# Decode attention and FFN on one core: weight loads with other layouts, a fourth buffer for K and for its transposes, and one score bank

## The chip, the cores and the metric

The kernel runs on one core of a Trainium2 chip. The metric is the device time of one execution in microseconds (us); six runs gave a median of 737.5 us, from 734.01 to 742.04. The core has a matrix engine (TensorE, PE in the profile; its weight loads are PEld), a vector engine (VectorE, DVE), a scalar engine (ScalarE, ACT), a general engine (GpSimd, POOL) and a sync engine (SP) that here issues every DMA. Each works through its own instructions in order and waits for others on semaphores. The data in HBM is moved by 16 DMA engines into the on-chip memory SBUF; TensorE writes its results into PSUM, which has 8 banks of 512 fp32 columns on 128 partitions.

## The reference

One decode step for 8 sequences. Layer norm, attention of one query token over a cache of 4096 keys, output projection, residual; then layer norm, an FFN with the mish activation, residual. All inputs are bfloat16.

```python
# x: (8, 1, 448)   k_cache, v_cache: (8, 8, 4096, 256)   wq: (448, 4096)   wo: (4096, 448)
# w1: (448, 1792)  b1: (1792,)  w2: (1792, 448)
q = (layernorm(x) @ wq)                  # 16 query heads of 256, two for each of 8 KV heads
scores = einsum("bhqd,bhkd->bhqk", q, k) * 256 ** -0.5
o = einsum("bhqk,bhkd->bhqd", softmax(scores), v)
h = x + o @ wo
hh = layernorm(h) @ w1 + b1
out = h + (hh * tanh(softplus(hh))) @ w2
```

K and V together are 268 MB; everything else is about 11 MB.

## The kernel before

**Pairs and groups.** The work is cut into 64 pairs (sequence b, KV head g), pair i having b = i % 8 and g = i // 8. Eight pairs with the same g form group j. Every pair needs 2.097 MB of K and 2.097 MB of V.

**One pair.** `kndma` loads K into one of three buffers `K_nat`, with the keys spread over the partitions (each partition takes 32 consecutive keys, 16 KB). `pe_T(i)`, called T(i) in the text, transposes it on TensorE in 64 matmuls against an identity (L609): 8 tiles of 1024 columns, each into one of three PSUM banks `kTp_ps`. `evac_task` copies each tile into one of three buffers `kT`, on ScalarE (L431) for every third tile and on VectorE (L436) for the other two. Tile t waits until tile t - 3 has been copied. `pe_qk(i)` then multiplies the transposed K with the two queries of the pair, 64 matmuls (L628) into the group's score bank. There are two score banks, `S_flat`, used by the groups in turn. `pe_pv(i)` multiplies V, in one of four buffers `vS`, with the weights of the softmax, 64 matmuls (L672), and ScalarE copies the output (L417).

**One group.** When the eight pairs of a group have their scores, a softmax chain goes back and forth between the engines. First half: VectorE takes the maxima (L480), TensorE transposes them (L643), VectorE reduces them (L486, L488), TensorE spreads them over the partitions (L646), VectorE copies (L491) and subtracts them from the scores (L493, which reads the score bank and signals `S_SCONS`). Then ScalarE takes the exponential (L403). Second half: VectorE sums (L501), TensorE sums over partitions (L652), VectorE takes the reciprocal (L504, L506), TensorE spreads it (L654) and VectorE scales (L511, L513, which signals `S_ET`). `pe_qtmm(g)` computes the queries of a KV head from wq (L586), `pe_attn(g)` multiplies the group's output with its part of wo (L688) and VectorE adds it (L527).

**The order.** Every task has a key, and each engine runs its tasks in the order of the keys: T(i) at i - 1.95, qk(i) at i, pv(i) at i + 11.5, the queries of KV head g at 8g - 0.7, the first half of the chain of group j at 8(j+1) - 0.42 on TensorE, its second half at 8(j+1) + 0.15. So T runs two pairs ahead of qk, and pv eleven pairs behind it. TensorE's order is, again and again: T(k), pv(k-13), qk(k-1), T(k+1) and so on.

**The loads.** All are issued by SP, in the order of keys of their own: K(i) at i - 2.55, V(i) at i + 10.5, wq of KV head g at 8g - 2.2 (two buffers), wo, then b1 at 58.8 and w1 and w2 at 62.05. Before each of them SP waits for its buffer: K(i) until the tiles of T(i-3) have been copied (`wait_evacs_before`, L250), V(i) until pv(i-4) is done (`S_PVDONE`), w1 and w2 until every tile of every T has been copied, since they go into the buffers of K. A load at the head of this order that must wait holds back all loads behind it. Between K(63) and the twelve last V loads, V(52) to V(63), stand w1 and w2.

**The weights' layouts.** wq comes in eight slices of 512 columns with row c x 112 + p on partition p, so 448 rows of 1 KB each. w1 is laid out the same way (448 rows of 3584 B), w2 with row c x 128 + p on partition p (1792 rows of 896 B), b1 as single elements of 2 B. The matmuls of the FFN's first layer are at L713, of its second at L721, and L718 is 36 matmuls without use between them.

Of the kernel before, what the change touches and what calls it, by code (L numbers as in the profile page):

```python
# [7 lines left out]
AF = mybir.ActivationFunctionType  # L8
AX = mybir.AxisListType

NKTP = 3
KN_ENGINES = ("sp", "sp", "sp")
V_ENGINE = "sp"
W_ENGINE = "sp"
N_WARM = 36
DSPLIT = False
EVAC_ENG = ("act", "dve", "dve")


def bass_sequential_preLN__gqa_block_cached__dense_activation_mish__decode_kernel(  # L20
# [43 lines left out]
    scale = float(Dh) ** -0.5  # L64
    EPS = 1e-5
    NKB = 3
    NVB = 4
    LAG = GP + 3

    def pair_bg(i):  # L70
# [3 lines left out]
    with ctx:  # L74
# [9 lines left out]

        kT = [sb([P, 2, Sk], dt.bfloat16) for _ in range(NKB)]
        vS = [sb([P, KH, KL * Dh], dt.bfloat16) for _ in range(NVB)]
        NKN = 3
        K_nat = [sb([P, KH, KL * Dh], dt.bfloat16) for _ in range(NKN)]
        wqbuf = [sb([DC, NDC, GW], dt.bfloat16) for _ in range(2)]
        KNSZ = KH * KL * Dh  # L90
        if NDC * F <= KNSZ and NFC * D <= KNSZ:
            w1_v = K_nat[0][0:DC, :, :].rearrange("p kh x -> p (kh x)")[:, 0:NDC * F].rearrange("p (c n) -> p c n", c=NDC)
# [32 lines left out]
        rstd = sb([B, 1], dt.float32)  # L125
        xnT_sb = sb([DC, NDC, B], dt.bfloat16)
        hnT_sb = sb([DC, NDC, B], dt.bfloat16)
        hb = sb([P, NFC, B], dt.float32)
        hmin = sb([P, NFC, B], dt.float32)
        hmax = sb([P, NFC, B], dt.float32)  # L130
        ea = sb([P, NFC, B], dt.float32)
        eb = sb([P, NFC, B], dt.float32)
        m_s1 = sb([P, NFC, B], dt.float32)
        m_num = sb([P, NFC, B], dt.float32)
        m_b2 = sb([P, NFC, B], dt.float32)
        m_den = sb([P, NFC, B], dt.float32)
        m_rden = sb([P, NFC, B], dt.float32)
        m_t = sb([P, NFC, B], dt.float32)
        actT = sb([P, NFC, B], dt.bfloat16)
        eps_t = sb([P, 1], dt.float32)  # L140
        lnv = sb([B, 1], dt.float32)

        S_flat = [ps([P, 512], dt.float32) for _ in range(2)]
        o_ps = ps([P, 512], dt.float32)
        misc_ps = ps([P, 512], dt.float32)
        p0_ps = ps([P, 512], dt.float32)
# [12 lines left out]
        qT_ps = misc_ps[:, 256:256 + NHC * B].rearrange("p (c b) -> p c b", c=NHC)  # L159
        xnT_ps = p0_ps[0:DC, 0:NDC * B // 2].bitcast(dt.bfloat16).rearrange("p (c b) -> p c b", c=NDC)  # L160
        attn_ps = p0_ps[0:B, 64:64 + D]
        h1T_ps = S_flat[1][:, 0:NFC * B].rearrange("p (c b) -> p c b", c=NFC)

        S_X = sem("s_x")
        S_WQ = [sem(f"s_wq{n}") for n in range(2)]
        S_V = [sem(f"s_v{n}") for n in range(NVB)]
        S_KN = [sem(f"s_kn{n}") for n in range(NKN)]
        S_WOB = [sem(f"s_wob{n}") for n in range(2)]
# [53 lines left out]
        def key_qtmm(g):  # L222
            return B * g - 0.7
# [45 lines left out]
        def w_events(eng):  # L269
            def wodma(g):  # L270
                if g >= 2:
                    eng.wait_ge(S_ATT, g - 1)
                eng.dma_start(
                    out=wobuf[g % 2][:, :, :],
                    in_=A_wo[g * GW:(g + 1) * GW, :].rearrange("(c p) n -> p c n", p=P),
                ).then_inc(S_WOB[g % 2], 16)

            def w12(_):
                wait_evacs_before(eng, NTBP * NP)
                eng.dma_start(out=w1_v, in_=B_w1.rearrange("(c p) f -> p c f", p=DC)).then_inc(S_W2, 16)  # L280
                eng.dma_start(out=w2_v, in_=B_w2.rearrange("(c p) n -> p c n", p=P)).then_inc(S_W2, 16)

            def b1load(_):
                with nc.allow_non_contiguous_dma(reason="tiny b1 transposed load"):
                    eng.dma_start(out=b1_sb[:, :], in_=B_b1.rearrange("(c p) -> p c", p=P)).then_inc(S_W2, 16)

            ev = []
            for g in range(Hkv):
                ev.append((min(key_attn(g), NP + LAG) - 4.0, 2, g, wodma))
            ev.append((key_T(NP - 1) + 1.0, 3, 0, w12))  # L290
            ev.append((key_qtmm(Hkv - 1) + 3.5, 4, 0, b1load))
            return ev
# [21 lines left out]
        def sp_prog(sp):  # L314
            def xload(_):
                sp.dma_start(out=x_bf[:, :], in_=A_x.rearrange("b o d -> (b o) d")).then_inc(S_X, 16)

            def wqload(g):
                if g >= 2:
                    sp.wait_ge(S_QTMM, g - 1)  # L320
                sp.dma_start(
                    out=wqbuf[g % 2][:, :, :],
                    in_=A_wq[:, g * GW:(g + 1) * GW].rearrange("(c p) n -> p c n", p=DC),
                ).then_inc(S_WQ[g % 2], 16)

            events = [(-10, 0, 0, xload)]
            for g in range(Hkv):
                events.append((key_qtmm(g) - 1.5, 5, g, wqload))
            for i in range(NP):
                if KN_ENG(i) == "sp":  # L330
                    events.append((key_T(i) - 0.6, 0, i, lambda i_: kndma(sp, i_)))
                if V_ENGINE == "sp":
                    events.append((key_pv(i) - 1.0, 1, i, lambda i_: vdma(sp, i_)))
            if W_ENGINE == "sp":
                events += w_events(sp)
            events.sort(key=lambda e: (e[0], e[1], e[2]))
            for key, kind, a, fn in events:
                fn(a)
            sp.wait_ge(S_H2, 1)
            sp.dma_start(out=out.rearrange("b o d -> (b o) d"), in_=h2_bf[:, :]).then_inc(S_OUT, 16)  # L340
            sp.wait_ge(S_OUT, 16)
# [223 lines left out]
        def pe_phase0a(pe):  # L565
            pe.wait_ge(S_XN, 1)
            pe.wait_ge(S_CONST, 1)
            for kc in range(NDC):
                ins = pe.matmul(xnT_ps[:, kc, :], lhsT=xn_bf[:, kc * DC:(kc + 1) * DC], rhs=ident_bf[0:B, 0:B],
                                is_transpose=True, start=True, stop=True)  # L570
            ins.then_inc(S_P0A, 1)

# [2 lines left out]
        def pe_qtmm(g):  # L575
            def f(pe):
                if g == 0:
                    pe.wait_ge(S_XNT, 1)
                pe.wait_ge(S_WQ[g % 2], 16 * (g // 2 + 1))
                ncb = n_chainB_before(key_qtmm(g))  # L580
                if ncb > 0:
                    pe.wait_ge(S_ET, ncb)
                for cc in range(4):
                    c = 4 * g + cc
                    for kc in range(NDC):
                        ins = pe.matmul(qT_ps[:, c, :], lhsT=wqbuf[g % 2][:, kc, cc * P:(cc + 1) * P],  # L586
                                        rhs=xnT_sb[:, kc, :], start=(kc == 0), stop=(kc == NDC - 1))
                ins.then_inc(S_QTMM, 1)
            return f
# [1 line left out]
        for g in range(Hkv):  # L591
            at("pe", key_qtmm(g), pe_qtmm(g))

        def pe_T(i):
            def f(pe):
                if i == 0:
                    pe.wait_ge(S_CONST, 1)
                pe.wait_ge(S_KN[i % NKN], 16 * NDMA * (i // NKN + 1))
                kn = K_nat[i % NKN]
                for tl in range(NTBP):  # L600
                    t = i * NTBP + tl
                    half, nb = divmod(tl, NTB)
                    if t >= NKTP:
                        wait_evac_of(pe, t - NKTP)
                    for jj in range(8):
                        blk = nb * 8 + jj
                        kh, kl = divmod(blk, KL)
                        c0 = kl * Dh + half * P
                        ins = pe.matmul(kTp_v[t % NKTP][:, jj * P:(jj + 1) * P], lhsT=kn[:, kh, c0:c0 + P],  # L609
                                        rhs=ident_bf[:, :], is_transpose=True, start=True, stop=True)  # L610
                    ins.then_inc(S_TB, 1)
            return f

        def pe_qk(i):
            b, g = pair_bg(i)
            j = i // GP
            c0 = (i % GP) * REP

            def f(pe):
                if i % GP == 0 and j >= 2:  # L620
                    pe.wait_ge(S_SCONS, j - 1)
                if i % B == 0:
                    pe.wait_ge(S_QT, g + 1)
                wait_evacs_before(pe, NTBP * (i + 1))
                kbuf = kT[i % NKB]
                for blk in range(NBLK):
                    for half in range(2):
                        ins = pe.matmul(  # L628
                            S_v[j % 2][:, blk, c0:c0 + REP],
                            lhsT=kbuf[:, half, blk * P:(blk + 1) * P],  # L630
                            rhs=qT_sb[:, b, half, REP * g:REP * g + REP],
                            start=(half == 0), stop=(half == 1),
                        )
                ins.then_inc(S_QKDONE, 1)
            return f

        def pe_chainA(j):
# [53 lines left out]
            return f  # L691

        for i in range(NP):
            at("pe", key_T(i), pe_T(i))
            at("pe", i, pe_qk(i))
            at("pe", key_pv(i), pe_pv(i))
        for j in range(NG):
            at("pe", key_chainA(j), pe_chainA(j))
# [4 lines left out]
        def pe_phase2(pe):  # L703
            pe.wait_ge(S_HN, 1)
            for kc in range(NDC):
                ins = pe.matmul(xnT_ps[:, kc, :], lhsT=hn_bf[:, kc * DC:(kc + 1) * DC], rhs=ident_bf[0:B, 0:B],
                                is_transpose=True, start=True, stop=True)
            ins.then_inc(S_P2_PE2ACT, 1)
            pe.wait_ge(S_HNT, 1)
            pe.wait_ge(S_W2, 3 * 16)  # L710
            for fc in range(NFC):
                for kc in range(NDC):
                    ins = pe.matmul(h1T_ps[:, fc, :], lhsT=w1_v[:, kc, fc * P:(fc + 1) * P], rhs=hnT_sb[:, kc, :],  # L713
                                    start=(kc == 0), stop=(kc == NDC - 1))
            ins.then_inc(S_P2_PE2DVE, 1)
            warm = kTp_ps[0][:, 0:P]
# [62 lines left out]
```

## Time and profile before

| | |
|---|---|
| median of 6 runs | 737.5 us (734.01 to 742.04) |
| the profiled execution | 737.96 us, its span 736.2 us |
| TensorE busy | 578.4 us (79%), mean granted clock 0.777 |
| VectorE, ScalarE, GpSimd busy | 272.6, 200.4, 1.4 us |
| HBM read | 279.00 MB, 379 GB/s over the span |
| DMA packets | 30587; under 512 B 4160, under 2 KB 13648 |
| L609 (transposes), L628 (qk), L672 (pv) busy | 340.4, 115.3, 115.1 us |
| K, V load from issue to landing (median) | 21.8, 26.4 us |

The profile gives the span, from the first to the last instruction, of one execution. Busy time counts an engine's instructions, not its waits. The granted clock is the share of TensorE's full speed that the chip allowed it. The DMA share is the mean busy share of the 16 DMA engines; it can be near 1 while few bytes move. A line of a group of instructions gives busy time, mean ns of one, then the idle time before them and what ended it. "issue" is idle time that ended with nothing that the profile shows. A line of a stretch of time gives its length, busy time and count for PE, PEld, DVE, ACT and POOL, then the granted clock, the DMA share and the GB/s. A line of the order of time gives start, duration, engine, line, operation and shape.

### The profile page before, as it was taken

To read this page: it belongs to the slowest core of one execution; us is meant where nothing else is said; L and a number is where in the kernel's file an instruction comes from. 1 tells how busy PE (TensorE), PEld (TensorE's weight loads), DVE (VectorE), ACT (ScalarE), POOL (GpSimd) and SP (SyncE) were. 2 spreads that over 40 slices of the span, in tenths; PEclk is the share of its full clock that TensorE was granted. 3 is DMA by queue.
4 is the path that set the end of the run, shared out by engine and by line. 5 is a ranking of instruction groups with operands and counts; after the bars stand their busy time and mean duration, and the time that the engine had idled before them with its cause. 6 is when DMAs were issued, how large, how long until landed. Compare 5 with 4: busy or idle time off the path is not lost.

```text
span 736.2 us, 26420 instructions
## 1 busy us (share of the span) xinstructions
PE 578.4 (79%) x12610; PEld 546.8 (74%) x12610; DVE 272.6 (37%) x450; ACT 200.4 (27%) x261; POOL 1.4 (0%) x11
## 2 busy tenths in 40 slices
PE   4998898779878899689888888868887888824436
PEld 4888798678777888689788787768887887723334
DVE  3554653253334443254323433325432533301003
ACT  2443442222223233132223232222221322200002
POOL 0000000000000000000000000000000000000000
PEclk9998898686888698787877788877977788855556
DMA  9998799999999999999999999999999988899990
GB/s 330 369 355 278 290 423 415 372 425 425 427 351 421 425 426 423 358 423 424 425 396 386 422 426 424 350 422 426 412 405 375 427 350 316 337 365 429 420 380 1
DMA packets 30587, 280.70 MB, mean 381 GB/s; under 512 B 4160, under 2 KB 13648, under 8 KB 14096
## 3 DMA queue, kind: packets, MB, share of 16 engines
q1 hardware_dynamic: 30480, 279.01, 94.4%
q8 instruction: 99, 1.62, 0.9%
q14 instruction: 8, 0.07, 0.0%
HBM read 279.00 MB, written 0.01 MB: 379 GB/s over the span
## 4 chain that ended last, share of the span: by engine, by line
PE 56%; DMA 28%; issue 6%; ACT 5%; DVE 4%; SPq 1%
PE ps L609 32%; DMA sb<-in_A_k_cache_dram 19%; PE ps L628 11%; PE ps L672 9%; DMA sb<-in_A_v_cache_dram 8%; ACT sb L431 5%; DVE sb L436 1%; DVE sb L501 1%; SPq L300 1%; PE ps L688 1%; PE ps L718 1%; PE ps L721 0%; PE ps L654 0%; PE ps L586 0%; DVE sb L486 0%
## 5 line engine op out<-in xcount | busy, mean ns | idle before, releaser
L609 PE MATMUL ps<-sb 128*128 128x128 bf16 x4096 | 340.4, 259 | 47.4 <-DMA sb<-in_A_k_cache_dram 24.1
L609 PEld LDWEIGHTS ps<-sb 128*128 128x128 bf16 x4096 | 316.6, 120 | 62.2 <-issue 23.5
L436 DVE COPY sb<-ps 128x1024 bf16<-128x1024 bf16 x341 | 227.5, 689 | 360.7 <-PE ps L609 358.9
L431 ACT ACTIVATE sb<-ps 128x1024 bf16<-128x1024 bf16 x171 | 174.9, 1023 | 353.7 <-PE ps L609 353.7
L672 PE MATMUL ps<-sb 128*128 128x16 bf16 x4096 | 115.1, 171 | 43.9 <-DMA sb<-in_A_v_cache_dram 42.5
L672 PEld LDWEIGHTS ps<-sb 128*128 128x128 bf16 x4096 | 110.7, 98 | 48.9 <-DMA sb<-in_A_v_cache_dram 43.9
L628 PE MATMUL ps<-sb 128*128 128x2 bf16 x4096 | 115.3, 164 | 33.0 <-issue 31.9
L628 PEld LDWEIGHTS ps<-sb 128*128 128x128 bf16 x4096 | 109.9, 97 | 34.9 <-issue 33.2
L417 ACT ACTIVATE sb<-ps 128x4 bf16<-128x4 f32 x64 | 12.0, 188 | 151.4 <-PE ps L672 151.4
L527 DVE TENSOR_TENSOR sb<-sb,ps 8x448 f32<-8x448 f32 x8 | 4.9, 608 | 53.3 <-PE ps L688 53.3
L652 PE MATMUL ps<-sb 128*16 128x1 f32 x16 | 1.6, 171 | 12.8 <-DVE sb L501 12.8
L652 PEld LDWEIGHTS ps<-sb 128*16 128x16 f32 x16 | 0.9, 96 | 14.1 <-DVE sb L501 14.1
L486 DVE TENSOR_REDUCE sb<-ps 16x1 f32<-16x128 bf16 x8 | 2.2, 279 | 20.9 <-PE ps L643 20.9
L688 PE MATMUL ps<-sb 128*8 128x448 bf16 x32 | 8.8, 407 | 0.6 <-ACT sb L417 0.6
L403 ACT ACTIVATE sb<-sb 128x512 f32<-128x512 f32 x8 | 5.0, 630 | 13.4 <-DVE sb L493 13.4
L501 DVE TENSOR_REDUCE sb<-sb 128x16 f32<-128x512 f32 x8 | 8.0, 998 | 0.7 <-ACT sb L403 0.7
L480 DVE TENSOR_REDUCE sb<-ps 128x16 bf16<-128x512 f32 x8 | 5.5, 683 | 6.2 <-PE ps L628 6.2
L654 PE MATMUL ps<-sb 16*128 16x16 f32 x16 | 3.6, 296 | 4.0 <-DVE sb L506 4.0
L654 PEld LDWEIGHTS ps<-sb 16*128 16x128 f32 x16 | 2.8, 215 | 4.8 <-DVE sb L506 4.8
L513 DVE TENSOR_TENSOR sb<-sb 128x512 bf16<-128x512 f32 x8 | 5.5, 692 | 0.3
L493 DVE TENSOR_TENSOR sb<-ps,sb 128x512 f32<-128x512 f32 x8 | 5.5, 691 | 0.3
L646 PE MATMUL ps<-sb 16*128 16x16 bf16 x8 | 1.4, 181 | 5.1 <-DVE sb L488 5.1
(58 smaller groups left out, 57.7 us busy)
## 6 DMA issues: line engine op xcount, KB each, us to landing
sb<-in_A_k_cache_dram SPq DMA_DIRECT2D x64, 2048.0 KB, 21.8
sb<-in_A_v_cache_dram SPq DMA_DIRECT2D x64, 2048.0 KB, 26.4
sb<-in_A_wq_dram SPq DMA_DIRECT2D x8, 448.0 KB, 28.7
sb<-in_A_wo_dram SPq DMA_DIRECT2D x8, 448.0 KB, 26.7
sb<-in_B_w_dram SPq DMA_DIRECT2D x2, 1568.0 KB, 11.7
sb<-in_A_x_dram SPq DMA_DIRECT2D x1, 7.0 KB
sb<-in_B_b_dram SPq DMA_DIRECT2D x1, 3.5 KB, 30.3
out_dram<-sb SPq DMA_DIRECT2D x1, 7.0 KB
```

The lines of the kernel that those rows point to most:

```text
L300: eng.dma_start(out=dst[:, :, :], in_=src).then_inc(semh, 16)
L417: act.activation(out=dst, in_=src, func=AF.Copy).then_inc(S_OCOPIED, 1)
L431: act.activation(out=dst, in_=src, func=AF.Copy).then_inc(S_EVA, 1)
L436: dve.tensor_copy(out=dst, in_=src).then_inc(S_EVD, 1)
L480: dve.tensor_reduce(out=M1[:, :], in_=S_vT[j % 2], axis=AX.X, op=ALU.max).then_inc(S_DVE2PE, 1)
L501: dve.tensor_reduce(out=R1[:, :], in_=E_f[:, :, :].rearrange("p k c -> p c k"), axis=AX.X, op=ALU.add).then_inc(S_DVE2PE, 1)
L609: ins = pe.matmul(kTp_v[t % NKTP][:, jj * P:(jj + 1) * P], lhsT=kn[:, kh, c0:c0 + P], rhs=ident_bf[:, :], is_transpose=True, start=True, s ...
L628: ins = pe.matmul(S_v[j % 2][:, blk, c0:c0 + REP], lhsT=kbuf[:, half, blk * P:(blk + 1) * P], rhs=qT_sb[:, b, half, REP * g:REP * g + REP] ...
L654: pe.matmul(RB_ps, lhsT=ones_f[0:NCOL, :], rhs=Dg2[:, :], start=True, stop=True).then_inc(S_PE2DVE, 1)
L672: ins = pe.matmul(OTacc[:, half * NCOL:(half + 1) * NCOL], lhsT=vb[:, kh, c0:c0 + P], rhs=ET[j % 2][:, blk, :], start=(blk == 0), stop=(bl ...
L688: ins = pe.matmul(attn_ps, lhsT=OT_sb[:, 4 * g + cc, :], rhs=wobuf[g % 2][:, cc, :], start=(cc == 0), stop=(cc == 2 * REP - 1))
L718: pe.matmul(warm, lhsT=ident_bf[:, :], rhs=ident_bf[:, :], start=(d == 0), stop=(d == N_WARM - 1))
```

## The change

The change has six parts.

1. wq is loaded in two halves of 2048 columns instead of eight slices, with row 4p + c on partition p (448 rows of 4 KB for each half). The second half goes into the same buffer, after the queries of KV head 3. The normalised x is picked with a step of 4 to match.
2. b1, w1 and w2 are laid out with partition p taking consecutive rows: 14 elements of b1, 4 rows of w1, 14 rows of w2. The FFN's first layer then reads its weights with a step of 14 elements (`fc:F:NFC`).
3. There are four K buffers instead of three, and three V buffers instead of four.
4. The K and V loads are issued in twos: K(2m) and K(2m+1) with the key of the first, V likewise. SP's order becomes V(2s-10), V(2s-9), K(2s+4), K(2s+5), again and again.
5. There are four banks for transposes instead of three; ScalarE copies one tile of four, VectorE three. The bank is taken from the scores, which now have one bank: qk of a new group waits until L493 of the group before has read it.
6. FFN temporaries lie in the space of the scores and exponentials, and the FFN's first result in another bank.

`pe_T` and `pe_qk` are also rewritten as generators, with a mode that interleaves them; it is switched off (`INTERLEAVE = False`), and the order of TensorE's instructions stays as it was.

```diff
-NKTP = 3
+NKTP = 4
+DGRP = 2
+INTERLEAVE = False
-EVAC_ENG = ("act", "dve", "dve")
+EVAC_ENG = ("act", "dve", "dve", "dve")
...
-    NVB = 4
+    NVB = 3
...
-        NKN = 3
+        NKN = 4
...
-        wqbuf = [sb([DC, NDC, GW], dt.bfloat16) for _ in range(2)]
+        HDH = HD // 2
+        wqh = sb([DC, NDC, HDH], dt.bfloat16)
...
-        S_flat = [ps([P, 512], dt.float32) for _ in range(2)]
+        S_one = ps([P, 512], dt.float32)
+        S_flat = [S_one, S_one]
...
-                eng.dma_start(out=w1_v, in_=B_w1.rearrange("(c p) f -> p c f", p=DC)).then_inc(S_W2, 16)
-                eng.dma_start(out=w2_v, in_=B_w2.rearrange("(c p) n -> p c n", p=P)).then_inc(S_W2, 16)
+                eng.dma_start(out=w1_v, in_=B_w1.rearrange("(p c) f -> p c f", c=NDC)).then_inc(S_W2, 16)
+                eng.dma_start(out=w2_v, in_=B_w2.rearrange("(p c) n -> p c n", c=NFC)).then_inc(S_W2, 16)
...
-                    eng.dma_start(out=b1_sb[:, :], in_=B_b1.rearrange("(c p) -> p c", p=P)).then_inc(S_W2, 16)
+                eng.dma_start(out=b1_sb[:, :], in_=B_b1.rearrange("(p c) -> p c", c=NFC)).then_inc(S_W2, 16)
...
-            def wqload(g):
-                if g >= 2:
-                    sp.wait_ge(S_QTMM, g - 1)
+            def wqload(hf):
+                if hf == 1:
+                    sp.wait_ge(S_QTMM, Hkv // 2)
                 sp.dma_start(
-                    out=wqbuf[g % 2][:, :, :],
-                    in_=A_wq[:, g * GW:(g + 1) * GW].rearrange("(c p) n -> p c n", p=DC),
-                ).then_inc(S_WQ[g % 2], 16)
+                    out=wqh[:, :, :],
+                    in_=A_wq[:, hf * HDH:(hf + 1) * HDH].rearrange("(p c) n -> p c n", c=NDC),
+                ).then_inc(S_WQ, 16)
...
-            for g in range(Hkv):
-                events.append((key_qtmm(g) - 1.5, 5, g, wqload))
+            events.append((key_qtmm(0) - 1.5, 5, 0, wqload))
+            events.append((key_qtmm(Hkv // 2) - 3.0, 5, 1, wqload))
             for i in range(NP):
+                i0 = (i // DGRP) * DGRP
                 if KN_ENG(i) == "sp":
-                    events.append((key_T(i) - 0.6, 0, i, lambda i_: kndma(sp, i_)))
+                    events.append((key_T(i0) - 0.6 + 0.001 * (i - i0), 0, i, lambda i_: kndma(sp, i_)))
                 if V_ENGINE == "sp":
-                    events.append((key_pv(i) - 1.0, 1, i, lambda i_: vdma(sp, i_)))
+                    events.append((key_pv(i0) - 1.0 + 0.001 * (i - i0), 1, i, lambda i_: vdma(sp, i_)))
...
-                if i % GP == 0 and j >= 2:
-                    pe.wait_ge(S_SCONS, j - 1)
+            if i % GP == 0 and j >= 1:
+                pe.wait_ge(S_SCONS, j)
...
-                    ins = pe.matmul(h1T_ps[:, fc, :], lhsT=w1_v[:, kc, fc * P:(fc + 1) * P], rhs=hnT_sb[:, kc, :],
+                    ins = pe.matmul(h1T_ps[:, fc, :], lhsT=w1_v[:, kc, fc:F:NFC], rhs=hnT_sb[:, kc, :],
```

## The prediction

> **What bounds the kernel now.** I read the slices and queues of the page first, then the same busy times in stretches of 18.4 us, then the waits, then the instructions in order of time.
>
> ```profile
> DMA  9998799999999999999999999999999988899990
> ```
> ```profile
> 55.20:73.60 18.40, 16.14 (x311) 15.32 (x309) 8.22 (x13) 6.14 (x6) 0.00 (x0) 0.81 0.85 278
> 73.60:92.00 18.40, 14.78 (x283) 13.84 (x281) 11.22 (x21) 7.60 (x9) 0.00 (x0) 0.86 0.77 289
> 184.00:202.40 18.40, 15.68 (x352) 14.55 (x350) 6.42 (x10) 4.73 (x7) 0.00 (x0) 0.82 1.01 427
> 202.40:220.80 18.40, 14.40 (x367) 13.91 (x365) 5.81 (x9) 5.22 (x7) 0.00 (x0) 0.87 1.02 352
> 607.20:625.60 18.40, 15.37 (x358) 14.43 (x359) 5.59 (x9) 4.47 (x6) 0.00 (x0) 0.81 0.84 313
> 644.00:662.40 18.40, 5.14 (x192) 4.98 (x189) 0.69 (x1) 0.19 (x1) 0.00 (x0) 0.57 1.04 362
> ```
>
> Each stretch ends with granted clock, DMA share and GB/s. There are three stages. Up to 92 us only K moves and TensorE sets the pace: the DMA is busy 0.77 to 0.85 at the end of it. From 92 to 588 us the DMA is full (about 1.0, 424 GB/s) except where a wq and a wo load pass: there it is just as busy and moves 352. From 642 us a tail is left (w1, w2, twelve V loads, then the FFN).
>
> ```profile
> SPq L250 <- DVE sb L436: 516.0, 61, 23.2
> ```
> ```profile
> PE ps L628 <- issue: 31.9, 17, 4.0
> PE ps L609 <- DMA sb<-in_A_k_cache_dram: 24.1, 11, 5.1
> PE ps L609 <- issue: 15.7, 13, 4.7
> PE ps L652 <- DVE sb L501: 12.8, 8, 2.7
> PE ps L609 <- ACT sb L431: 7.1, 35, 0.2
> ```
>
> The SP queue's own wait shows what releases the K loads: the evacuation of an earlier T, 61 times. The other waits say that TensorE is nearly a second bound. In the order of time, T(13) (the transposes of pair 13) begins at 102.2 and T(58) at 570.9: 468.7 us for 45 pairs. The waits for K or V over 1 us in between are 4.58, 1.70, 1.43, 1.04, 2.35, 3.64 and 3.52 us, 18.3 together; without them TensorE needs 450.4/45 = 10.0 us a pair. The DMA needs two times 2.097 MB at 424 GB/s, 9.9 us, and an eighth of a wq and a wo load. So the full DMA sets the middle, but no more than 18.3 us can be won there before TensorE takes over.
>
> **Part 1, the loads of wq.** Eight loads of 448 packets of 1 KB become two of 448 packets of 4 KB. Price: in 202 to 221 us the lost bytes are (425 - 352) x 18.4 / 425 = 3.2 us for 448 + 512 packets (wq and wo), 3.3 ns a packet, so 1.5 us for each set of 448. Six of the eight loads lie in the full stretch, one of the two new ones will: 5 x 1.5 = 7.5 us less DMA time. The Trainium skill ("DMA: Bandwidth & Descriptors", Specifications) speaks against this: from 512 B up a transfer should run at line rate, so 1 KB packets would have nothing to win and this part would be 0. The row with 352 GB/s at a share of 1.02 says otherwise; I take the row.
>
> **Part 2, four K buffers and loads in pairs.** Today V(0) is issued after T(10) is evacuated, at 87.2 us (K(13) just before it). The new order is V, V, K, K, and K(13), V(0), V(1) all follow the evacuation of T(9), at about 73 us (T(9) starts at 71.6 now; it comes some 3 us earlier, Part 3). By then K(0) to K(12) and half of wq, 29.1 MB, are issued and about 28.3 moved with the code; at 424 GB/s that is 66.7 us of transfer, so 6.3 us are lost at the start. Now, by 92 us, the five stretches have moved (330 + 369 + 356 + 278 + 289) x 18.4 us = 29.8 MB, 70.3 us of transfer: 21.7 us lost. Less the part of wq brought forward (0.92 MB, 2.2 us) the DMA runs 13 us ahead from there. The middle of the DMA side: -13 - 7.5 = -20.5 us.
>
> In the steady state I find no deeper queue. Just before V(2s-9) is issued, after T(2s+1) and pv(2s-12), K up to 2s+3 and V up to 2s-10 are out; today, at the same place, also K(k+2) and V(k-11). The fourth K buffer is used up by the pairing, and the third V buffer is just enough.
>
> **Part 3, TensorE's side.** A fourth transpose bank removes the 0.2 us waits on L431; a T at full clock loses two or three of them, and I count 0.3 us since VectorE now copies three tiles of four (3 x 0.67 us against 4 x 0.50 on TensorE, a near tie). The single score bank costs a wait, seen in this group:
>
> ```profile
> 320.54 0.18 PE L646 MATMUL ps<-sb 16*128 16x16 bf16 x1 [0.63 <-DVE sb L488]
> 320.75 1.75 PE L628 MATMUL ps<-sb 128*128 128x2 bf16 x64
> 320.75 0.17 DVE L491 COPY sb<-ps 128x16 f32<-128x16 f32 x1 [0.27 <-PE ps L646]
> 320.96 0.69 DVE L493 TENSOR_TENSOR sb<-ps,sb 128x512 f32<-128x512 f32 x1
> ```
>
> L628 of the next group now starts beside the subtraction; it will have to wait for its end at 321.65: 1.0 us, seven times. Behind it on TensorE stand the next T and the second half of the chain, so their evacuations and the SP queue's K load slide with it. As T's last tile is now always VectorE's, L501 starts later too: 0.4 us a group. Up to T(13): 1 us earlier at the first T (K(0) no longer shares with wq), 11 x 0.3, and 1.4 back for one group: -3. From there: six groups +8.4, the rest of L431's waits -3.7, the data waits -18.3. Sum -16.6 us. The DMA could give 20.5, TensorE takes 16.6; since a late K and a late T still alternate I leave 1 us of waits: T(58) comes 15.5 us earlier.
>
> The code fetch stays: the "issue" waits of 31.9 and 15.7 us fall at shifting places inside a run of 64 matmuls, 256 instructions apart or a multiple. The skill ("Runtime: NRT & Kernel Launch", Instruction fetch mechanics) has these crossings of 16 KB blocks mostly hidden. By the rule TensorE would need 1 us less a pair and the DMA's 20.5 us would all come through; by the rows it doesn't.
>
> **Part 4, b1.** Its 1792 packets of 2 B become 128 of 28 B.
>
> ```profile
> 588.94 0.43 SPq L285 DMA_DIRECT2D sb<-in_B_b_dram  x1
> 601.45 11.07 SPq L300 DMA_DIRECT2D sb<-in_A_k_cache_dram  x1
> 612.57 4.89 SPq L300 DMA_DIRECT2D sb<-in_A_v_cache_dram  x1
> ```
>
> The queue stands 16 us behind it and the stretch falls to 313 GB/s. Yet T(59) to T(63) take 595.0 to 635.6, 10.1 us a pair, TensorE's own pace; and w1 and w2 wait for T(63)'s evacuation at 642.15 with the DMA idle before. The jam is hidden: -0.5 us (a little of the 3.0 us code wait). Were TensorE not there, it would be 8 us.
>
> **Part 5, w1 and w2.** 448 + 1792 packets become 112 + 128. The stretch from 644 us loses (425 - 362) x 18.4 / 425 = 2.7 us, and a little before it: -3 us, wholly in the tail's chain (V(52) is behind them). The tail keeps its pace with three V buffers: V(i) is issued 2 us after V(i-3) lands, with 2 x 4.9 - 2 = 7.8 us still queued.
>
> **Part 6, strided weights of the FFN.** L713's 56 weight loads now step 28 B. No row has a strided load on TensorE.
>
> ```profile
> L501 DVE TENSOR_REDUCE sb<-sb 128x16 f32<-128x512 f32 x8 | 8.0, 998 | 0.7 <-ACT sb L403 0.7
> L513 DVE TENSOR_TENSOR sb<-sb 128x512 bf16<-128x512 f32 x8 | 5.5, 692 | 0.3
> L713 PE MATMUL ps<-sb 112*128 112x8 bf16 x56 | 1.7, 168 | 0.3 <-ACT sb L450 0.3
> ```
>
> L501 reads with a 64 B step and takes 1.44 times L513: 0.44 x 1.7 = 0.7 us. Upper end: 998/512 = 1.95 ns an element, 128 of them, 56 times, 14 - 1.7 = 12 us. A gain is excluded, it is the same work. I take +2, nearer the measured ratio. The FFN temporaries in old tiles, hn's 8 B step (4 loads) and the score bank moved for L713 cost nothing: same operations, at a place where nothing else runs.
>
> **Sum.** -15.5 - 0.5 - 3 + 2 = -17 us on 737.96 us of the profiled execution (span 736.2 and 1.8 around it): 721. The median of the runs shown, 737.5, is 0.5 less. Below about 0.5% (733.8 to 741.2 us) a measurement of this kernel can't tell a change.
>
> **Rivals.**
> (a) TensorE takes all the gain: for the lead of 13 us speaks an idle DMA, against it that TensorE needs 10.0 us a pair. If its clock sinks by 3% of 450 us (13 us) with fewer rests, the end is at about 734.
> (b) The opposite: the half clock comes after waits (0.50 granted from 592 to 600 us, after the wait to 594.9), and a T then takes 6.4 us instead of 4.4. With 18 us of waits gone, six or seven T fewer at half clock: 13 us more, 708.
> (c) Slower: the third V buffer. V(2s-9) waits for pv(2s-12) and holds back the two K loads behind it on the SP queue. In the steady state they still have 10 us in hand (issued at 20s+17.5, landed by 20s+30, used at 20s+40), and one pair lands 5 to 7 us late on its slowest engine now. If TensorE slips more than about 4 us further, the DMA runs dry once in two pairs; 1 us each over 26 double pairs is 26, and -17 becomes +9: 747. For it: the queue order. Against: the depth equals today's, where the DMA stays full.
> (d) It doesn't do what it says: the pairing undoes the fourth buffer at the start as well; then only Parts 1, 5 and 6 remain, 7.5 + 3 - 2 less 1.4 x 7 for the chain, plus 7 for L431: 732.
>
> **How the numbers follow.** Forecast 0.53 (its own range 712 to 730); (a) 0.12, half of it within 0.5%; (b) 0.10; (c) 0.18; (d) 0.07, all faster but for a third. Faster 0.73, same 0.09, slower 0.18. The range goes from (b), 707, to 744, which leaves out most of (c), and holds the 12 us of Part 6.
>
> **What would show it.** Right: the DMA share at 1.0 from about 73 us; 420 GB/s with one dip instead of six from wq; L609's waits for K below 8 us; L628 waiting for L493 1.0 us seven times; T(63)'s copies done near 626 us; no K issue of 11 us after b1. Wrong: DMA shares under 0.95 between 100 and 580 us, V waits of L672 before the tail, SP waiting long for L672, or L713 over 4 us.

## The result and the profile after

The changed kernel takes 724.83 us (median of 8 runs, 721.42 to 729.29) against 738.1 for the kernel before: a ratio of 0.9825, 95% interval 0.979 to 0.986, so 13 us less and clear of the noise. The forecast was 721.0 us, in a range of 707 to 744. The profiled execution took 723.04 us, its span 721.3.

First the slices of the changed kernel's page: the DMA share and the GB/s.

```profile
DMA  8999999999999999999999999999999999499970
GB/s 308 401 426 364 393 410 417 422 426 421 424 416 424 402 386 346 427 420 430 419 415 404 428 392 413 429 423 424 401 420 423 424 380 405 135 395 426 426 322 1
```

The dips before 92 us are gone. One deep dip has come: slice 35, from 613 to 631 us, where the share falls to 0.4. Next the same time in four stretches, up to T(13), up to the seventh group's end, up to the issue of w1, and the tail. Of the kernel before:

```profile
0.00:102.00 102.00, 81.81 (x1634) 77.36 (x1635) 51.54 (x84) 39.89 (x42) 1.40 (x11) 0.92 0.89 334
102.00:571.00 469.00, 394.79 (x8595) 377.46 (x8592) 181.05 (x290) 132.34 (x171) 0.00 (x0) 0.79 1.01 408
571.00:642.00 71.00, 59.16 (x1275) 56.14 (x1275) 29.21 (x48) 21.39 (x27) 0.00 (x0) 0.80 0.90 366
642.00:717.00 75.00, 29.43 (x944) 26.64 (x940) 4.99 (x12) 3.07 (x14) 0.00 (x0) 0.53 0.98 393
```

Of the changed kernel:

```profile
0.00:102.00 102.00, 78.76 (x1638) 77.31 (x1639) 55.19 (x93) 30.94 (x33) 1.40 (x11) 0.90 0.97 381
102.00:555.00 453.00, 386.22 (x8576) 376.23 (x8574) 195.85 (x319) 103.17 (x142) 0.00 (x0) 0.79 1.00 414
555.00:626.00 71.00, 58.13 (x1322) 56.55 (x1319) 31.90 (x53) 16.42 (x22) 0.00 (x0) 0.81 0.85 348
626.00:701.00 75.00, 28.64 (x916) 25.91 (x912) 4.91 (x11) 3.07 (x14) 0.00 (x0) 0.52 0.97 392
```

T(13) begins at 102 us in both, although the DMA has moved (381 - 334) x 102 us = 4.8 MB more by then. The middle is 16 us shorter. From there to the issue of w1 both take 71 us, and the tail 75. So the whole gain arises in the middle. The waits of the changed kernel say what went and what came:

```profile
PE ps L632 <- issue: 30.5, 17, 2.9
PE ps L614 <- issue: 21.3, 16, 2.6
PE ps L685 <- DVE sb L506: 16.5, 8, 2.7
PE ps L632 <- DVE sb L498: 7.0, 7, 1.0
PE ps L614 <- DMA sb<-in_A_k_cache_dram: 6.8, 2, 4.0
PE ps L592 <- DMA sb<-in_A_wq_dram: 3.0, 1, 3.0
```

L614 is the transposes (L609 before), L632 qk, L685 and L506 the second half of the chain, L498 the subtraction. The waits for K fell from 11 (24.1 us) to two, both before 28 us. The ring waits for ScalarE's copies are gone. The single score bank's wait is there, seven times. SP's own waits have changed places:

```profile
SPq L304 <- PE ps L705: 516.6, 59, 16.3
SPq L255 <- DVE sb L441: 103.6, 13, 16.5
```

It now stands at the V loads (L304, for a pv) instead of at the K loads (L255). No wait of TensorE comes of it: from the landings in the trace, half of K(13) to K(57) lie at least 8.8 us in SBUF before their T begins, against 1.8 us before; for V it is 14.1 us against 2.6.

### The profile page after: what moved, and what is told of

Its sections match the earlier page's. It is cut to its first block, busy times and chain, and to the rows that moved or that the text cites. A ratio compares the mean times of both kernels' runs of the same rounds, so it can differ in the third digit from the quotient of the medians.

```text
span 721.3 us, 26414 instructions
## 1 busy us (share of the span) xinstructions
PE 565.7 (78%) x12610; PEld 546.6 (76%) x12610; DVE 293.6 (41%) x493; ACT 157.3 (22%) x218; POOL 1.4 (0%) x11
## 4 chain that ended last, share of the span: by engine, by line
PE 72%; DMA 13%; issue 8%; DVE 6%; SPq 0%; ACT 0%; ACTq 0%
PE ps L614 42%; PE ps L632 14%; PE ps L705 13%; DMA sb<-in_A_v_cache_dram 9%; DMA sb<-in_A_k_cache_dram 3%; DVE sb L441 2%; PE ps L721 1%; DVE sb L506 1%; DVE sb L498 1%; PE ps L752 0%; PE ps L687 0%; PE ps L760 0%; PE ps L592 0%; DVE sb L491 0%; DVE sb L493 0%
## 5 line engine op out<-in xcount | busy, mean ns | idle before, releaser
L441 DVE COPY sb<-ps 128x1024 bf16<-128x1024 bf16 x384 | 248.9, 687 | 325.2 <-PE ps L614 324.2
L614 PE MATMUL ps<-sb 128*128 128x128 bf16 x4096 | 326.9, 258 | 29.8 <-issue 21.3
L614 PEld LDWEIGHTS ps<-sb 128*128 128x128 bf16 x4096 | 314.5, 119 | 32.6 <-issue 29.6
L436 ACT ACTIVATE sb<-ps 128x1024 bf16<-128x1024 bf16 x128 | 131.1, 1025 | 310.7 <-PE ps L614 310.7
L632 PE MATMUL ps<-sb 128*128 128x2 bf16 x4096 | 115.7, 164 | 37.9 <-issue 30.5
L632 PEld LDWEIGHTS ps<-sb 128*128 128x128 bf16 x4096 | 110.4, 98 | 39.9 <-issue 31.8
L685 PE MATMUL ps<-sb 128*16 128x1 f32 x16 | 1.6, 171 | 16.5 <-DVE sb L506 16.5
L685 PEld LDWEIGHTS ps<-sb 128*16 128x16 f32 x16 | 0.9, 95 | 17.8 <-DVE sb L506 17.8
L506 DVE TENSOR_REDUCE sb<-sb 128x16 f32<-128x512 f32 x8 | 8.0, 998 | 0.7 <-ACT sb L408 0.7
L592 PE MATMUL ps<-sb 112*128 112x8 bf16 x128 | 4.5, 167 | 3.8 <-DMA sb<-in_A_wq_dram 3.0
L592 PEld LDWEIGHTS ps<-sb 112*128 112x128 bf16 x128 | 4.1, 98 | 4.1 <-issue 4.1
## 6 DMA issues: line engine op xcount, KB each, us to landing
sb<-in_A_k_cache_dram SPq DMA_DIRECT2D x64, 2048.0 KB, 18.3
sb<-in_A_v_cache_dram SPq DMA_DIRECT2D x64, 2048.0 KB, 14.3
```

What stands on the lines that cost most here:

```text
L436: act.activation(out=dst, in_=src, func=AF.Copy).then_inc(S_EVA, 1)
L441: dve.tensor_copy(out=dst, in_=src).then_inc(S_EVD, 1)
L506: dve.tensor_reduce(out=R1[:, :], in_=E_f[:, :, :].rearrange("p k c -> p c k"), axis=AX.X, op=ALU.add).then_inc(S_DVE2PE, 1)
L592: ins = pe.matmul(qT_ps[:, c, :], lhsT=wqh[:, kc, cl:cl + P], rhs=xnT_sb[:, kc, :], start=(kc == 0), stop=(kc == NDC - 1))
L632: ins = pe.matmul(S_v[j % 2][:, blk, c0:c0 + REP], lhsT=kbuf[:, half, blk * P:(blk + 1) * P], rhs=qT_sb[:, b, half, REP * g:REP * g + REP] ...
```

## The experiments

Each kernel was measured beside the kernel before on the same chip. "Ratio" is to that kernel; where two of the kernels are compared, the difference of their ratios counts, 0.01 being 7.4 us. In the table all but the ratio comes from one profiled execution: T(13)'s start; from there to T(57)'s start; from T(57) to the issue of w1; the summed time of all DMA packets over 16 engines; and the DMA's idle time before T(13) and from T(57) to the last V (from the packets' times, in steps of 0.5 us).

| kernel | ratio (95%) | T(13) | to T(57) | to w1 | DMA sum | idle start, end |
|---|---|---|---|---|---|---|
| before | 1 | 102.2 | 468.7 | 71.3 | 702.1 | 12.8, 9.8 |
| changed | 0.9825 (0.979 to 0.986) | 102.1 | 453.2 | 70.4 | 685.2 | 4.4, 13.2 |
| e1 eight wq slices | 0.9933 (0.989 to 0.998) | 100.2 | 459.9 | 73.6 | 695.5 | 4.8, 13.2 |
| e2 two score banks | 0.9851 (0.981 to 0.989) | 107.5 | 453.0 | 70.0 | 686.8 | 6.6, 12.9 |
| e3 no pairs | 0.9911 (0.988 to 0.994) | 107.2 | 456.3 | 69.9 | 687.3 | 7.6, 15.7 |
| e4 early w1, w2 | 0.9813 (0.977 to 0.985) | 105.1 | 453.4 | 54.0 | 686.5 | 6.1, 5.2 |
| e5 old buffers | 0.9968 (0.993 to 1.000) | 105.8 | 460.2 | 73.0 | 690.9 | 13.6, 14.3 |
| e6 buffers alone | 0.9917 (0.988 to 0.995) | 100.0 | 457.9 | 74.9 | 699.1 | 3.8, 10.4 |
| e7 layouts alone | 0.9971 (0.994 to 1.000) | 105.7 | 462.9 | 72.7 | 692.5 | 12.8, 15.1 |
| e9 rows on 128 | 0.9802 (0.977 to 0.984) | 102.7 | 453.8 | 67.3 | 680.7 | 6.0, 10.7 |
| e10 128, eight slices | 0.9798 (0.975 to 0.985) | 100.9 | 454.0 | 70.5 | 680.6 | 7.1, 12.5 |
| e11 128, early w1, w2 | 0.9732 (0.970 to 0.976) | 104.1 | 452.9 | 52.2 | 681.1 | 7.1, 3.6 |
| e12 as e11, eight slices | 0.9730 (0.969 to 0.977) | 99.3 | 459.9 | 52.7 | 682.3 | 5.8, 5.1 |

Three pairs of rows run the same instructions up to the issue of w1, and so show how far single executions differ: changed and e4 by 3.0 us at T(13), e9 and e11 by 1.4, e10 and e12 by 1.6 there and by 5.9 us in the middle. Where below a gain is placed by one profile, differences of this size say nothing; the ratios, from several runs, are the firmer evidence.

**e1, wq in eight slices again.**

```diff
...
-            events.append((key_qtmm(0) - 1.5, 5, 0, wqload))
-            events.append((key_qtmm(Hkv // 2) - 3.0, 5, 1, wqload))
+            for g in range(Hkv):
+                events.append((key_qtmm(g) - 1.5, 5, g, wqload))
...
```

> The changed kernel with wq in eight slices of 1 KB rows again (rows 4p+c kept). Theory (TensorE is the bound from 28 to 626 us, the DMA has 8.8 us in hand at the median K): no loss in the middle, and T(2) no longer waits for half of wq in front of K(2), so it begins some 3 us earlier: 721 to 726 us. Rival (the fewer wq packets won the time, as the prediction's Part 1 had it): 7 us slower, 732.

733.04 us, so the rival holds: the halves are worth 8 us in this kernel. T(2) did begin earlier, at 21.7 us instead of 27.9, and 2 us were left of it at T(13); the middle gave back 7 us and the way to w1 another 3. Waits for K do not show it (4.5 us in all, two). The DMA sum does: 695.5 us against 685.2. Of these 10 us only 2 are the wq packets themselves (16.7 against 14.5 us); the rest is that the K and V packets take 634 ns in the mean instead of 626. The packets show where: in the middle, those that start while a slice of wq is being moved take 883 ns in the mean, all others 622. How the longer DMA time becomes 8 us of time is not shown, since TensorE has no wait for K or V in e1's middle; there its own work is longer (396.4 us against 386.5) and its waits for code ("issue") are shorter (40.9 against 46.2), together 4.6 us more, where e10 and e12 differ by 7.1 in this sum.

**e2, three transpose banks and two score banks.**

```diff
-NKTP = 4
+NKTP = 3
...
-EVAC_ENG = ("act", "dve", "dve", "dve")
+EVAC_ENG = ("act", "dve", "dve")
...
-        S_one = ps([P, 512], dt.float32)
-        S_flat = [S_one, S_one]
+        S_flat = [ps([P, 512], dt.float32) for _ in range(2)]
...
```

> The changed kernel with three transpose banks and two score banks, ScalarE copying every third tile, as before. Theory: the waits of L632 for L498 (7.0 us) and the longer L506 waits (some 4) go, the 0.2 us waits for the tile copies (7 us) come back: within 4 us of 725. Rival (the fourth bank won the time): 733 or more.

725.44 us: no difference that can be told. The exchange of a score bank for a transpose bank pays itself back. In e2's waits the ring waits stand again where the score bank's wait was:

```profile
PE ps L613 <- ACT sb L435: 6.8, 33, 0.2
PE ps L684 <- DVE sb L505: 13.7, 8, 2.7
```

6.8 + 13.7 = 20.5 us here, 7.0 + 16.5 = 23.5 us in the changed kernel.

**e3, loads one by one.** `DGRP = 1`.

> The changed kernel with K and V loads issued one by one (four K, three V buffers kept). Theory: V(0) still follows the copies of T(9), since K(13) waits for T(9) with four K buffers, so the lead is kept: 722 to 727 us. Rival (the pairing gives the lead): 732 or more.

730.9 us, near the rival's figure. What the profile shows is a loss at the very start: without pairs wq's 1.8 MB stand between K(0) and K(1), not behind both. TensorE's first instructions in e3 and in the changed kernel:

```profile
10.17 5.24 PE L614 MATMUL ps<-sb 128*128 128x128 bf16 x64 [5.02 <-DMA sb<-in_A_k_cache_dram]
22.66 5.81 PE L614 MATMUL ps<-sb 128*128 128x128 bf16 x64 [7.25 <-DMA sb<-in_A_k_cache_dram]
```

```profile
9.29 10.03 PE L614 MATMUL ps<-sb 128*128 128x128 bf16 x128 [4.03 <-DMA sb<-in_A_k_cache_dram]
22.38 0.57 PE L592 MATMUL ps<-sb 112*128 112x8 bf16 x16 [3.05 <-DMA sb<-in_A_wq_dram]
```

T(1) begins at 22.7 us in e3 and at 15.6 in the changed kernel (whose first row holds T(0) and T(1) together); at T(13) 5 us are left, and the middle is 3 us longer, the latter within the spread of single executions.

**e4, w1 and w2 two transposes earlier.** With four K buffers, the two that w1 and w2 go into were last used by K(60) and K(61).

```diff
-                wait_evacs_before(eng, NTBP * NP)
+                wait_evacs_before(eng, NTBP * (NP - 2))
```

> The changed kernel with w1 and w2 issued after the copies of T(61) instead of T(63): with four K buffers the two that they go into were last used by K(60) and K(61). Theory: the DMA's idle time of some 10 us before the w1 issue (share 0.10, 0.02, 0.37 from 616 to 628) is on the path, since the tail is DMA work: 715 to 718 us. Rival (w1, w2 and V(52) then delay K or V of the last pairs, or the tail hangs on TensorE): 723 to 728.

720.42 us. The idle time after T(57) falls from 13.2 to 5.2 us; the time is 4 us shorter by the medians and 1 us by the ratios, less than expected, and its interval overlaps that of the changed kernel. e11 below tells it more clearly.

**e5, three K and four V buffers, no pairs.**

```diff
...
-DGRP = 2
+DGRP = 1
...
-    NVB = 3
+    NVB = 4
...
-        NKN = 4
+        NKN = 3
```

> The changed kernel with three K and four V buffers and single loads, as before; all else as changed. Theory (the lead of the DMA from the fourth K buffer removed 18 us of waits for K and V): those waits come back, 734 to 738 us. Rival (layouts and banks won it): 724 to 728.

735.09 us: the buffers and pairs are worth 10 us in this kernel. The time fell where the theory had it, the reason did not. There are again only two waits for K, both at the start:

```profile
PE ps L614 <- DMA sb<-in_A_k_cache_dram: 11.4, 2, 6.2
```

What came back is the DMA's idle time at the start (13.6 us), 4 us at T(13) and 7 us in the middle, which there is TensorE's own time: its work between T(13) and T(57), waits taken off, is 394.3 us instead of 386.4. The 10 us are clear of the noise, from ten runs; that they are TensorE's own time rests on this one execution, and why it should need more is not shown.

**e6, the buffers and pairs alone, in the kernel before.** The reverse of e5's diff, in the other kernel.

> The kernel before with four K and three V buffers and paired loads, nothing else changed. Theory: nearly the whole gain, 722 to 728 us. Rival (the buffers alone do little, since b1 and the eight wq loads still slow the DMA): 732 to 738.

731.74 us: 6 us of the 13 by the ratio. The start's idle time falls to 3.8 us, as in the changed kernel. But the DMA sum stays at 699.1 us, and late in the middle K is short again: K(48), K(56), K(58) and K(62) land as their T begins, and five waits for K remain:

```profile
PE ps L611 <- DMA sb<-in_A_k_cache_dram: 10.7, 5, 4.3
```

**e7, the layouts alone.** e5's and e2's diffs together.

> The changed kernel with the buffers, pairs and banks of before: only the layouts of wq, b1, w1 and w2 (and the places of the FFN's temporaries) are changed. Theory: the wq packets took 16.4 us of 16 engines before and take 14.5 after, w1 and w2 the same as before; b1's jam is hidden; the strided weights cost 1.9: 734 to 739 us. Rival (layouts won it): 724 to 729.

737.3 us, 0.9971 with an interval that reaches 1.000: some 2 us, and perhaps none. The DMA sum fell by 9.6 us, yet it idles 5 us more after T(57), waits for K of 6.7 us are in the middle again, the first T come later (wq before K(1)), and the strided weights cost 2. The two add up to more than their parts: 2 and 6 us alone, 13 together (e2 shows that the banks give nothing). By the three intervals the extra is 5 us, give or take 4.

**e8, the same bytes over 128 partitions.** w1 and wq are read as flat blocks, so the queries and the FFN use shuffled weights.

```diff
...
-                    out=wqh[:, :, :],
-                    in_=A_wq[:, hf * HDH:(hf + 1) * HDH].rearrange("(p c) n -> p c n", c=NDC),
+                    out=wqF[:, :, 0:1792],
+                    in_=A_wq[hf * 224:(hf + 1) * 224, :].rearrange("d n -> (d n)").rearrange("(p c n) -> p c n", p=P, c=NDC),
...
```

> The changed kernel with the same bytes of w1 and of each wq half loaded over 128 partitions instead of 112 (w1 in 128 packets of 12544 B, a wq half in 512 packets of 3584 B); the weights then lie in other places, so the FFN and the queries are computed from shuffled weights. Theory (a load over 112 partitions is slow per byte, whatever its packets): w1's packets fall from 899 ns to some 480, wq's from 266 ns to under 170. Rival (the rows or their place in HBM make them slow): w1's stay above 750 ns. The time as a whole within 3 us of the changed kernel.

w1's packets fall from 899 (14336 B) to 473 ns (12544 B), wq's from 266 (4 KB) to 140 ns (3.5 KB). In the changed kernel itself w2, over 128 partitions, takes 474 ns for 12544 B. So it is the spread over 112 partitions that is slow; e9 shows it again with the rows as they were. The single run took 712.62 us, more of a gain than expected; the next run, with the products computed as they should be, did not repeat it.

**e9, 448 rows as three blocks of 128 and one of 64.**

```diff
...
+    KP = [128, 128, 128, D - 384]
...
+                sp.dma_start(out=wqh[:, 0:3, :], in_=A_wq[0:384, cs].rearrange("(c p) n -> p c n", p=P)).then_inc(S_WQ, 16)
+                sp.dma_start(out=wqh[0:64, 3, :], in_=A_wq[384:448, cs]).then_inc(S_WQ, 16)
...
-                                        rhs=xnT_sb[:, kc, :], start=(kc == 0), stop=(kc == NDC - 1))
+                                        rhs=xnT_sb[0:KP[kc], kc, :], start=(kc == 0), stop=(kc == NDC - 1))
...
```

> The changed kernel with the 448 rows of wq and w1 on 128 partitions (three blocks of 128 rows and one of 64, each half of wq and w1 in two DMAs), the products computed as before. Theory (the DMA is full from T(13) to T(57) and its summed busy time, 685 us in the changed kernel, sets the end): wq's 4 KB packets fall from 266 to some 160 ns, the K and V packets beside them are no longer slowed, the sum falls by about 9 us: 712 to 717 us. Rival (TensorE alone paces the middle, and a shorter DMA time is hidden): 721 to 727.

722.61 us: the packets are as expected (159 ns for 4 KB), the DMA sum is 4.5 us smaller, and the middle is as long as in the changed kernel, 453.8 us. The rival holds: at 10.3 us a pair TensorE is the limit, and a shorter DMA time beyond that point is hidden.

**e10, the same in eight slices.**

> As the run with rows on 128 partitions, but wq in eight slices of 1 KB rows. Theory (the cost of wq is that of 112 partitions, not that of the number of packets): the 1 KB packets take some 50 ns instead of 74, and the time stays within 4 us of the run with halves: 711 to 719 us. Rival (the number of packets costs, as eight slices over 112 partitions cost 8 us): 721 or more.

723.61 us, the same as e9. On 128 partitions the 1 KB packets take 46 ns instead of 74, the K and V packets beside them 671 ns instead of e1's 883, and eight slices cost nothing more than two halves. But two halves over 112 partitions cost nothing either that can be told (the changed kernel against e9). So e1's loss takes both, eight slices and 112 partitions; neither alone shows it.

**e11, e9 and e4 together; e12, with eight slices as well.**

> Rows on 128 partitions, and w1 and w2 issued after the copies of T(61). Theory: the two gains add, the DMA's idle time after T(57) falls from 13 to 5 us: 706 to 712 us, the shortest yet. Rival (the early w1 and w2 only push V(52) back): the same as rows on 128 alone, 713 to 717.

> As the one before it, with wq in eight slices. Theory: K(2) no longer waits behind 1.8 MB of wq, so T(2) begins near 22 instead of 25 to 28 us, but the DMA is the bound and moves the same bytes: within 3 us of the run with halves, 706 to 713 us. Rival (an earlier start carries to the end): 703 to 706.

717.12 and 716.98 us: 5.5 us below e9 (5 by the ratios), the intervals apart, and e12 as far below e10. So the wait of w1 and w2 was on the path. The stretch from 555 to 626 us of e11 beside its DMA:

```profile
555.00:626.00 71.00, 60.87 (x1327) 59.11 (x1324) 30.89 (x52) 16.61 (x23) 0.00 (x0) 0.78 0.98 396
```

The share is 0.98 where the changed kernel had 0.85. SP issues w1 at 609.2 us instead of 625.7. In e12 T(2) begins at 21.3 us instead of 25.4; the two medians are the same, so nothing of it reaches the end. (At T(57) e12's profile is the later one, 559.2 against 557.0 us, but e10's, with the same start, is at 554.9.) Both beat the two kernels of this case; e11 is 2.7% below the kernel before.

## Why the prediction was right, and where its steps were not

The total was right: -17 us forecast, -13 measured by the medians and -15 between the two profiled executions. The size of the main term was right too, T(57) comes 15.6 us earlier where 15.5 was forecast. That it fits so closely is in part luck: the forecast had 3 us of it before T(13) and 12.5 in the middle, and all of it came in the middle. (The text called that instruction T(58); counted through, the T that begins at 570.9 us is T(57), so TensorE's pace was 450.4/44 = 10.2 us a pair, not 10.0.) The steps, from the two profiled executions:

| step | forecast, us | measured, us |
|---|---|---|
| T(13) earlier | -3 | -0.1 |
| waits for K and V, T(13) to T(57) | -18.3, 1 left | -20.1 (to 0) |
| score bank and later chain | +8.4 | +6.7 |
| ring waits on L431 | -3.7 | -3.4 (to 0) |
| code waits ("issue") | 0 | +10.1 (36.1 to 46.2) |
| TensorE's own work | 0 | -8.7 (395.2 to 386.5) |
| b1, w1 and w2, up to the last V | -3.5 | -0.9 |
| strided weights, FFN | +2 | +1.9; the whole end after the last V +1.5 |

*The waits and the chain* (Part 3) went as forecast, down to the seven waits of 1.0 us for the subtraction. Code waits and own work, which the forecast left alone, changed much each and by 1.4 us together (431.3 to 432.7). So in these two executions the middle's gain is that of the forecast's three terms: -20.1, +6.7 and -3.4. (Its 18.3 counts only waits over 1 us.)

*T(13).* The step failed at the order of the first loads. The forecast let K(0) gain 1 us because wq no longer shares with it, and did not ask what stands behind wq: K(2), which lands at 27.9 us instead of 21.8. T(2) begins 3.5 us later, and this eats what the fourth bank gave. (e4, the same up to there, has its T(13) 3.0 us later still.)

*The lead of the DMA* (Part 2) was sized at 13 us. By 102 us it is 4.8 MB, 11.3 us at 424 GB/s, less the 2.2 us of wq brought forward: 9 us. The direction and place were right (e5, e6), though the full chain "lead, therefore no waits" is shown only in part: e5 lost 10 us without one wait for K in the middle.

*wq* (Part 1) has about the right size by the wrong price. Forecast -7.5 us of DMA time by 3.3 ns for each packet; e1 shows 10 us of it and 8 us of time. But e10 shows that on 128 partitions the number of packets costs no time. The row of 352 GB/s was right to overrule the skill's rule on 512 B that the forecast cites; it did not say which property of the load made it slow, and I chose the packet count.

*w1 and w2* (Part 5) failed for the same reason: the step priced packets, not partitions. Their packets became 240, and the 112 of w1 take 899 ns for 14336 B, where 16384 B of K take 611. From the issue of w1 to pv(52) it is 18.6 us, 19.1 before: -0.5 instead of -3.

*The strided weights* (Part 6): 56 matmuls from 1.66 to 3.52 us. The group's line was 168 ns a matmul; it is now

```profile
L752 PE MATMUL ps<-sb 112*128 112x8 bf16 x56 | 3.5, 201 | 0.3 <-ACT sb L455 0.3
```

*The wait of w1 and w2.* The forecast noted that they wait for T(63) with the DMA idle before, and stopped there. With the DMA further ahead the idle time from T(57) to the last V grew from 9.8 to 13.2 us, and e11 shows 5 us of it on the path (e4 1 to 4).

*The rivals.* (c), the third V buffer, did not happen: there is no wait of pv for V before the tail. (a) and (b) were both about the clock, which stayed at 0.79 in the middle: the waits for data went, but with the code waits and the chain's TensorE's idle share there fell only from 16 to 15%. (The stretch that (b) quotes is no example of its rule: the half clock was granted from 591.9 us, the wait began at 592.4. The direction is in the traces, though. From 100 to 640 us the clock falls to half 39 times in each kernel, and in the 3.4 us ahead of a fall TensorE is idle 26% of the time in the kernel before and 33% in the changed one, against 8 and 9% where the clock stays full.) (d) fell: with the pairs the DMA's idle time at the start is 4.4 us, before 12.8.

*What stays open.* TensorE's own work between T(13) and T(57) ranges from 383 to 402 us over these traces, with the granted clock of the same stretch between 0.77 and 0.80, and its code waits from 36 to 46 us. Both spreads are of the size of the gain, and I found no rule by which a kernel gets the one or the other, or their sum (431 to 440 us, e8 left out). So the split of the middle's 15.5 us holds for these two executions only: the runs show that the parts give the gain, but not by which of TensorE's times in general. Nor was b1 tried alone.

## What to carry to other kernels

When two resources need nearly the same time for each step (here TensorE's 10.2 us a pair, and a full DMA at 10.7), price every part against both and do not take a part's worth from a test of it alone: 2 and 6 us became 13. When loads are merged, look at what stands behind the merged one in its queue at the start. Price a slow load by packets of several sizes and of several partition counts before calling it a matter of size.

## What the runs showed of the hardware

A load over 112 partitions was slow for every byte at each of three packet sizes; over 128 (or 128, 128, 128 and 64) it was not. Median times of packets in the traces:

| bytes in a packet | 112 partitions | 128 partitions |
|---|---|---|
| 1024 | 74 ns (e1) | 46 ns (e10) |
| 4096 | 266 ns (changed) | 159 ns (e9) |
| 14336; 12544 | 899 ns (changed) | 473 ns (e8) |

That is 14 to 16 bytes per ns over 112 partitions and 22 to 27 over 128, where the 16 KB packets of K have 27. The 899 ns is one execution's; in the other runs with w1 in 112 packets it lies between 770 and 985.

It slows others too: the 16 KB packets of K and V that start beside a wq slice over 112 partitions take 883 ns in the mean (e1), beside one over 128 partitions 671 (e10), all others 622 and 623. Why 112 is slow was not tried.

TensorE's waits that end with nothing in the profile ("issue") are waits for its code: between 20 and 640 us all those over 0.4 us, 28 in the kernel before and 34 in the changed one, end 1.2 to 1.6 us after a 16 KB packet of the instruction queue q8 has landed, and such packets come only every 7 us. The line is the same for both kernels:

```profile
q8 instruction: 99, 1.62, 0.9%
```

These waits did not fall with the waits for data, but are 36.1 us of the middle before and 46.2 after.
